# Converting w_out on one line with w_in, and reading it back from DRAM in the first gated pass

## The chip, the cores and the metric

The kernel runs on one core of one Trainium2 chip. The metric is the device time of one execution in microseconds. Three executions of the kernel before took 993.34, 993.7 and 997.28 us; the median is 993.7 us.

## What is computed

Sparse attention over 4 batches and 8 heads (sequence 768, head size 64), and behind it a gated two-layer block over all 3072 tokens (model size 512, hidden size 2048). The mask holds a window of neighbouring blocks of 32, the first and the last block, and three sampled blocks for each row of blocks.

```python
scores = scale * np.matmul(q, k.transpose(0, 1, 3, 2))
scores = np.where(mask, scores, -1000000000.0)
scores = scores - np.max(scores, axis=-1, keepdims=True)
attn = np.exp(scores)
attn = attn / (np.sum(attn, axis=-1, keepdims=True) + 1e-09)
x = np.matmul(attn, v)                      # heads side by side: 3072 x 512
...
h = x @ w_in
g = np.where(h >= 1, h, np.where(h <= -1, 0.0, (h + 1) ** 2 / 4))
out = g @ w_out
```

The weights w_in (512 x 2048) and w_out (2048 x 512) arrive in float64, as 64-bit words.

## The kernel before

**Attention.** The 32 heads follow one another, 12 steps each; a step is one tile of 128 keys by 384 queries. Each head first takes the maximum of its scores: 12 matmuls (L267), 12 reductions on VectorE (L272), a join (L276), a transpose on TensorE (L280) and a product that writes the row of negative maxima into the head's query tile QA (L283). Then come its scores (L303 and L304), the exponential on ScalarE (L308) and the product with v. Heads 0 to 9 are "whole": exponentials go to TensorE in float32 in one matmul (L333). From head 10 on they are split into a rounded part and a rest (L196 on ScalarE, L316 on VectorE), take two matmuls (L335 and L336), and are summed on GpSimd (L323). q and k are loaded (L214), rounded, and moved by DMA into the tiles QA, KA, QB and KB (L221, L237, L238).

**The gated block.** For each batch there are two passes, one for each half of its queries, that run beside the attention of the next batch. A pass goes over 16 slices fi of 128 hidden units, three steps each. The first layer (L457 to L459) multiplies x, in two parts, with w_in's slice, in two parts, from the resident tile wi. Then ScalarE and VectorE form g: L463, L466, L469 (VectorE), a rounding (gh, L196) and a rest (gl, L478, VectorE). The second layer (L485 to L487) multiplies gh and gl with w, the slice fi of w_out, in two parts of 128 x 512.

**Conversions.** Each tile of 128 x 512 float64 weights becomes a float32 pair of a rounded part and a rest. `convert` places three pieces: the load (L162, queue of SP, 512 KB into a tile raw, three buffers), the bits (L168 on ScalarE, then L169, L170, L172 and L174 on VectorE, into a tile cva, two buffers), and the split (a rounding on ScalarE, L196, and a subtraction on GpSimd, L180). There are 16 tiles of w_in and 16 of w_out.

- w_in's tiles stand on a line of their own: one every CSTEP = 5.75 steps from step 8 on. Their split goes into wi.
- w_out's tiles stand in the first gated pass (`first`, batch 0, first half): slice fi is converted shortly ahead of its use, straight into the tile w that the second layer reads, and then stored to a DRAM copy wo_dram (L448, queue of SP, 512 KB). The other seven passes load w back from there (L441), one slice of three steps ahead. The tiles w of conversions and of loads come from one pool of three buffers, wst.

**What sets the order.** Every piece is put into a list with a due time in steps, the list is sorted by it, and the instructions are recorded in that sequence; a scheduler then fixes one order for each engine. Each engine, and SP's queue of DMAs, works in its order: an instruction that waits holds up all behind it.

```python
    for t, load, bits, split in sorted(conv, key=lambda x: -x[0]):
        last = t = min(t, last - P["cd"])
        at(t - P["cl"], load)
        at(t, bits)
        at(t + P["cs"], split)
```

Of the kernel before, what the change touches and what calls it, by code (L numbers as in the profile page):

```python
# [9 lines left out]
F32R = mybir.dt.float32r  # L10
# [12 lines left out]
DM, FF = 512, 2048  # L23
# [14 lines left out]
def body(ctx, tc, qk_t, v, sampled_blocks, moe_w_in, moe_w_out, ind, cm, negd, ident, fold, out):  # L38
# [13 lines left out]
    wst = pool("wst", 3)  # L52
# [13 lines left out]
    Q_KEEP = nc.sync  # L66
# [6 lines left out]
    def f(ap):  # L73
        return ap.bitcast(F32)
# [10 lines left out]
    wi = cst.tile([128, 4, 2, FF], F32R, name="wi")  # L85
# [43 lines left out]
    def at(t, fn, *args):  # L129
        plan.append((t, fn, args))  # L130
# [26 lines left out]
    def convert(t, src, dst, done=None):  # L157
        st = {}

        def load():  # L160
            st["raw"] = cv.tile([128, 512, 2], I32, name="raw", bufs=3)
            Q_RAW.dma_start(out=st["raw"], in_=src.bitcast(I32).rearrange("p (c w) -> p c w", w=2))  # L162

        def bits():
            raw = st["raw"]
            lo32, hi32 = raw[:, :, 0], raw[:, :, 1]
            a = st["a"] = cv.tile([128, 512], I32, name="cva", bufs=2)
            nc.scalar.activation(out=f(a), in_=f(hi32), func=AF.Abs)  # L168
            nc.vector.tensor_scalar(out=f(a), in0=f(a), scalar1=CLO, scalar2=CHI, op0=ALU.max, op1=ALU.min)  # L169
            nc.vector.tensor_scalar(out=a, in0=a, scalar1=3, scalar2=0x3FFFFFFF,  # L170
                                    op0=ALU.logical_shift_left, op1=ALU.bitwise_and)
            nc.vector.scalar_tensor_tensor(out=a, in0=hi32, scalar=-0x40000000, in1=a,  # L172
                                           op0=ALU.bitwise_and, op1=ALU.bitwise_or)
            nc.vector.scalar_tensor_tensor(out=a, in0=lo32, scalar=29, in1=a,  # L174
                                           op0=ALU.logical_shift_right, op1=ALU.bitwise_or)

        def split():
            hi, lo = dst()
            rounded(CH, hi, f(st["a"]))
            nc.gpsimd.tensor_tensor(out=lo, in0=f(st["a"]), in1=f(hi), op=ALU.subtract)  # L180
            if done:
                done()

        conv.append((t, load, bits, split))
# [247 lines left out]
    wo_dram = dr.tile([NF, 128, 2 * DM], F32R, name="wo_dram")  # L432

    def moe(t0, p, b, hf, first):

        g = {}
        G = {**P, **PM} if first else P

        def w_load(fi):
            w = g["w", fi] = wst.tile([128, 2, DM], F32R, name="w")  # L440
            Q_W.dma_start(out=f(w.rearrange("p a d -> p (a d)")), in_=f(wo_dram[fi]))  # L441

        def w_dst(fi):
            w = g["w", fi] = wst.tile([128, 2, DM], F32R, name="w")
            return w[:, 0], w[:, 1]

        def w_keep(fi):
            Q_KEEP.dma_start(out=f(wo_dram[fi]), in_=f(g["w", fi].rearrange("p a d -> p (a d)")))  # L448

        def l1(fi, j):  # L450
            if j == 0:
                last = b == B - 1 and fi % 2
                g["h", fi] = psa.tile([128, 512], F32, name="pa") if last else psh.tile([128, 512], F32, name="hp")
            hv = g["h", fi][:, 0:HALF]
            x = xt[b, j, hf]
            fs = slice(fi * 128, (fi + 1) * 128)
            nc.tensor.matmul(out=hv, lhsT=wi[:, j, 0, fs], rhs=x[:, 0], start=(j == 0), stop=False)  # L457
            nc.tensor.matmul(out=hv, lhsT=wi[:, j, 0, fs], rhs=x[:, 1], start=False, stop=False)  # L458
            nc.tensor.matmul(out=hv, lhsT=wi[:, j, 1, fs], rhs=x[:, 0], start=False, stop=(j == NP - 1))  # L459

        def g_relu(fi):
            r = g["r", fi] = mt.tile([128, HALF], F32, name="r")
            nc.scalar.activation(out=r, in_=g["h", fi][:, 0:HALF], func=AF.Relu, bias=half_c, scale=0.5)  # L463

        def g_sq(fi):
            nc.scalar.activation(out=g["r", fi], in_=g["r", fi], func=AF.Square)  # L466

        def g_max(fi):
            nc.vector.scalar_tensor_tensor(out=g["r", fi], in0=g["r", fi], scalar=1.0, in1=g["h", fi][:, 0:HALF],  # L469
                                           op0=ALU.min, op1=ALU.max)  # L470

        def g_hi(fi):
            gh = g["gh", fi] = mt.tile([128, HALF], F32R, name="gh", bufs=3)
            rounded(nc.scalar, gh, g["r", fi])

        def g_lo(fi):
            gl = g["gl", fi] = mt.tile([128, HALF], F32R, name="gl", bufs=3)
            (nc.gpsimd if first and fi % 4 in GL1 else nc.vector).tensor_tensor(out=gl, in0=g["r", fi], in1=f(g["gh", fi]), op=ALU.subtract)  # L478

        def l2(fi, t):  # L480
            if fi == 0:
                g["o", t] = psc.tile([128, DM], F32, name=f"oa{t}")
            ts = slice(t * 128, (t + 1) * 128)
            gh, gl, w, o = g["gh", fi], g["gl", fi], g["w", fi], g["o", t]
            nc.tensor.matmul(out=o, lhsT=gh[:, ts], rhs=w[:, 0], start=(fi == 0), stop=False)  # L485
            nc.tensor.matmul(out=o, lhsT=gh[:, ts], rhs=w[:, 1], start=False, stop=False)  # L486
            nc.tensor.matmul(out=o, lhsT=gl[:, ts], rhs=w[:, 0], start=False, stop=(fi == NF - 1))  # L487

        end = b == B - 1 and hf == 1
        dst = out[b * S:(b + 1) * S].rearrange("(p t) m -> p t m", t=T)  # L490

        def o_copy(t):
            if t == 0:
                g["out"] = op.tile([128, 3, DM], F32, name="o")
            if end and t == 1:
                nc.vector.tensor_copy(out=g["out"][:, t], in_=g["o", t])
            else:
                nc.scalar.copy(out=g["out"][:, t], in_=g["o", t])
            if end:
                Q_OUT.dma_start(out=dst[:, hf * 3 + t], in_=g["out"][:, t])  # L500

        def o_store():
            if not end:
                Q_OUT.dma_start(out=dst[:, hf * 3:hf * 3 + 3], in_=g["out"])

        for fi in range(NF):
            u = t0 + fi * p
            if first:
                convert(u + 1.5 * p - P["co"], moe_w_out[fi * 128:(fi + 1) * 128, :], lambda fi=fi: w_dst(fi),
                        lambda fi=fi: w_keep(fi))  # L510
            else:
                at(u - p, w_load, fi)
            for j in range(NP):
                at(u + j * p * G["l1"], l1, fi, j)
            m = u + p / 2
            at(m + G["gr"], g_relu, fi)
            at(m + G["gs"], g_sq, fi)
            at(m + G["gm"], g_max, fi)
            at(m + G["gh"], g_hi, fi)
            at(m + G["gl"], g_lo, fi)  # L520
            for t in range(3):
                at(u + G["l2"] * p + t * p * G["l3"], l2, fi, t)
        for t in range(3):
            at(t0 + (NF + G["l2"] - 1) * p + (t + 1) * p * G["l3"] + 0.05, o_copy, t)
        at(t0 + (NF + 1) * p + 0.1, o_store)
# [8 lines left out]
    begin = [PER * H * (b + 1) + DELAY for b in range(B + 1)]  # L534
    p = PER * H / (2 * NF)
    for b in range(NMOE):
        for hf in range(2):
            moe(begin[b] + hf * NF * p, p, b, hf, b == 0 and hf == 0)
    for fq in range(4):
        for kt in range(4):  # L540
            cs = slice(fq * 512, (fq + 1) * 512)
            convert(CONV + (4 * fq + kt) * CSTEP, moe_w_in[kt * 128:(kt + 1) * 128, cs],
                    lambda kt=kt, cs=cs: (wi[:, kt, 0, cs], wi[:, kt, 1, cs]))
    plan_conversions()
    plan.sort(key=lambda x: x[0])
    early = [x for x in plan if x[0] < MANUAL]
# [8 lines left out]
P = {'vw': 4.0, 'r1': 0.857, 'r2': 4.031, 'qs': 9.647, 'ks': 11.666, 'vs': 9.131, 'ld': 5, 'm0': 7.832, 'm1': 5.0, 'mr': 0.46, 'mc': 2.3, 'mt': 1.325, 'mw': 0.9, 'ex': 0.524, 'ph': 1.22, 'pl': 1.349, 'ps': 0.841, 'ow': 0.704, 'ot': 0.2, 'oa': 0.549, 'ah': 0.3, 'al': 0.578, 'su': 0.637, 'de': 1.414, 'yw': 0.799, 'yy': 2.173, 'xm': 0.774, 'xh': 1.0, 'xl': 2.518, 'gr': 0.1, 'gs': 0.279, 'gm': 0.314, 'gh': 0.934, 'gl': 1.232, 'l2': 1.494, 'l3': 0.158, 'l1': 0.121, 'cl': 9.0, 'cs': 1.705, 'cd': 1.8, 'co': 5.196, 'lag': 3.5}  # L555
# [16 lines left out]
NHEADS = B * H  # L572
NMOE = B
PER = 2 * T
CONV, CSTEP = 8.0, 5.75
CLO, CHI = (struct.unpack("<f", struct.pack("<I", w))[0] for w in (0x38100000, 0x47EFFFFF))

_INS = ["qk_t", "v", "sampled_blocks", "moe_w_in", "moe_w_out"]
# [49 lines left out]
```

## Time and profile before

| | |
|---|---|
| median of three executions | 993.7 us |
| the profiled execution, its own time | 991.61 us |
| its span, first to last instruction | 989.8 us |
| TensorE busy | 947.2 us (96%) |
| weight loads (PEld) busy | 830.4 us (84%) |
| VectorE (DVE) busy | 735.9 us (74%) |
| ScalarE (ACT) busy | 637.2 us (64%) |
| GpSimd (POOL) busy | 323.5 us (33%) |
| DMA moved | 154.43 MB |
| first matmul of the gated block (L457) | at 157.2 us |
| conversions on VectorE, first and last | at 20.5 and 284.9 us |

Shares are over the whole span and mix stages with different limits, so they tell little about a change that touches the first 290 us. That stretch is read from sums over parts of it. Matmuls overlap each other, so TensorE's busy time is no measure of how much it could still take; the count of matmuls in a stretch, with the time of one in a stretch where nothing holds TensorE up, is a better one. A row of waits names the engine and line that waited, and what it waited for.

### The profile page before, as it was taken

What the parts mean: (1) busy time and instruction counts of PE and PEld (TensorE: products, weight loads), DVE (VectorE), ACT (ScalarE), POOL (GpSimd) and SP (SyncE); (2) the same over time, 40 slices, a digit from 0 to 9 for tenths busy, and PEclk for the clock granted to TensorE, in tenths of its full rate; (3) what the DMA queues carried; (4) which work ended last, traced back from release to release, by engine and by line L of the source; (5) the groups of instructions that cost most, each with busy time, mean ns of one, the idle gap of its engine ahead of it and who ended that gap; (6) DMA issues with size and microseconds to landing.
All of it is one profiled execution on the core that took longest, in us unless ns stands there. A gap on an engine that the chain in (4) does not pass through costs nothing.

```text
span 989.8 us, 14583 instructions
## 1 busy us (share of the span) xinstructions
PE 947.2 (96%) x4687; PEld 830.4 (84%) x4687; DVE 735.9 (74%) x1349; ACT 637.2 (64%) x1302; POOL 323.5 (33%) x283
## 2 busy tenths in 40 slices
PE   5898899999899999999999999999999999999998
PEld 3666567778779989999989999998999899899996
DVE  5888887679998887888888897888888885422222
ACT  3676666666667666777767676866777676533433
POOL 1222120225554344444544444344544444000000
PEclk9999999999999999999999999999999999999999
DMA  6666676753455454656455454655546442434442
GB/s 196 200 182 184 190 207 204 228 180 103 155 170 172 128 141 129 186 151 174 136 143 175 133 150 137 184 158 152 156 130 187 116 124 86 154 128 128 160 128 96
DMA packets 56216, 154.43 MB, mean 156 GB/s; under 512 B 9612, under 2 KB 17952, under 8 KB 56140
## 3 DMA queue, kind: packets, MB, share of 16 engines
q1 hardware_dynamic: 56100, 153.48, 52.1%
q8 instruction: 37, 0.61, 0.3%
q14 instruction: 39, 0.32, 0.1%
q10 hardware_dynamic: 40, 0.03, 0.0%
HBM read 100.92 MB, written 14.81 MB: 117 GB/s over the span
## 4 chain that ended last, share of the span: by engine, by line
PE 70%; DVE 7%; ACT 2%; issue 1%; POOL 0%; POOLq 0%; ACTq 0%; DVEq 0%
PE oa L485 8%; PE oa L487 8%; PE oa L486 8%; PE hp L457 7%; PE hp L458 7%; PE hp L459 7%; PE po L335 5%; PE pa L303 4%; PE pa L304 4%; PE po L336 4%; PE pa L267 4%; DVE pl L316 2%; DVE mc L272 1%; PE pa L459 1%; PE pa L458 1%
## 5 line engine op out<-in xcount | busy, mean ns | idle before, releaser
L323 POOL TENSOR_TENSOR acc<-acc,pt 128x384 f32<-128x384 f32 x176 | 206.6, 1174 | 189.9 <-ACT pt L308 146.2
L272 DVE TENSOR_REDUCE mc<-pa 128x1 f32<-128x384 f32 x384 | 203.3, 549 | 20.4 <-PE pa L267 17.1
L196 ACT CAST ph<-pt 128x384 fp32r<-128x384 f32 x264 | 135.8, 514 | 94.4 <-PE po L335 90.1
L316 DVE TENSOR_TENSOR pl<-pt,ph 128x384 fp32r<-128x384 f32 x264 | 166.9, 632 | 33.3 <-ACT ph L196 32.4
L308 ACT ACTIVATE pt<-pa 128x384 f32<-128x384 f32 x288 | 140.5, 489 | 49.6 <-PE pa L304 41.6
L457 PE MATMUL hp<-x,wi 128*128 128x384 f32 x448 | 156.3, 349 | 5.4 <-DVE r L469 5.3
L485 PE MATMUL oa<-w,gh 128*128 128x512 f32 x384 | 153.3, 399 | 0.3 <-ACT gh L196 0.3
L459 PE MATMUL hp<-x,wi 128*128 128x384 f32 x448 | 152.1, 340 | 0.0
L458 PE MATMUL hp<-x,wi 128*128 128x384 f32 x448 | 152.0, 339 | 0.0
L487 PE MATMUL oa<-w,gl 128*128 128x512 f32 x384 | 151.5, 394 | 0.0
L486 PE MATMUL oa<-w,gh 128*128 128x512 f32 x384 | 150.8, 393 | 0.0
L267 PE MATMUL pa<-KA,QA 88*128 88x384 f32 x384 | 139.4, 382 | 8.8 <-DMA QA<-qkh 5.9
L469 DVE SCALAR_TENSOR_TENSOR r<-r,hp 128x384 f32<-128x384 f32 x112 | 61.8, 552 | 74.6 <-ACT r L466 74.4
L478 DVE TENSOR_TENSOR gl<-r,gh 128x384 fp32r<-128x384 f32 x128 | 91.0, 711 | 30.2 <-ACT gh L196 28.1
L267 PEld LDWEIGHTS pa<-KA,QA 88*128 88x128 f32 x384 | 73.4, 193 | 33.2 <-DVE mc L272 11.2
L303 PE MATMUL pa<-QA,KA 102*128 102x384 f32 x288 | 99.7, 346 | 0.7 <-DVE mc L272 0.4
L463 ACT ACTIVATE r<-hp,half_c 128x384 f32<-128x384 f32 x112 | 65.1, 581 | 52.3 <-PE hp L459 49.2
L304 PE MATMUL pa<-QB,KB 128*128 128x384 f32 x288 | 98.3, 341 | 0.0
L335 PE MATMUL po<-ph,vn 128*128 128x384 f32 x264 | 91.9, 348 | 4.7 <-DVE xun L345 3.9
L457 PEld LDWEIGHTS hp<-x,wi 128*128 128x128 f32 x448 | 85.0, 190 | 12.3 <-DVE r L469 7.8
L323 POOL TENSOR_TENSOR acc<-pt 128x384 f32<-128x384 f32 x44 | 45.6, 1037 | 136.7 <-ACT pt L308 132.9
L336 PE MATMUL po<-pl,vn 128*128 128x384 f32 x264 | 88.8, 336 | 0.0
(97 smaller groups left out, 1665.7 us busy)
## 6 DMA issues: line engine op xcount, KB each, us to landing
w<-wo_dram SPq DMA_DIRECT2D x112, 512.0 KB
qk<-in_qk_t_dram SPq DMA_DIRECT2D x32, 384.0 KB
raw<-in_moe_w_in_dram SPq DMA_DIRECT2D x16, 512.0 KB
raw<-in_moe_w_out_dram SPq DMA_DIRECT2D x16, 512.0 KB
wo_dram<-w SPq DMA_DIRECT2D x16, 512.0 KB
lv<-in_v_dram SPq DMA_DIRECT2D x32, 192.0 KB
KA<-qkh SPq DMA_DIRECT2D x32, 192.0 KB
QA<-qkh SPq DMA_DIRECT2D x32, 192.0 KB
```

The costliest lines, as they stand in the source:

```text
L267: nc.tensor.matmul(out=pm[:, 0:HALF], lhsT=QAi[0:KM, t * 128:(t + 1) * 128], rhs=KAi[0:KM, kh * HALF:(kh + 1) * HALF], start=True, stop=True)
L272: nc.vector.reduce_max(out=st["mc"][:, t, kh:kh + 1], in_=st.pop(("pm", t, kh))[:, 0:HALF], axis=AX.X)
L308: nc.scalar.activation(out=p, in_=st.pop(("ps", c))[:, 0:HALF], func=AF.Exp, scale=SCALE)
L316: (nc.gpsimd if i < 2 * H and c in PL1 else nc.vector).tensor_tensor(out=pl, in0=st["p", c], in1=f(st["ph", c]), op=ALU.subtract)
L323: nc.gpsimd.tensor_tensor(out=st["acc", hf], in0=prev, in1=st["p", c], op=ALU.add)
L335: nc.tensor.matmul(out=po, lhsT=st["vn"][:, c], rhs=st["ph", c], start=(c == 0), stop=False)
L457: nc.tensor.matmul(out=hv, lhsT=wi[:, j, 0, fs], rhs=x[:, 0], start=(j == 0), stop=False)
L458: nc.tensor.matmul(out=hv, lhsT=wi[:, j, 0, fs], rhs=x[:, 1], start=False, stop=False)
L459: nc.tensor.matmul(out=hv, lhsT=wi[:, j, 1, fs], rhs=x[:, 0], start=False, stop=(j == NP - 1))
L485: nc.tensor.matmul(out=o, lhsT=gh[:, ts], rhs=w[:, 0], start=(fi == 0), stop=False)
L486: nc.tensor.matmul(out=o, lhsT=gh[:, ts], rhs=w[:, 1], start=False, stop=False)
L487: nc.tensor.matmul(out=o, lhsT=gl[:, ts], rhs=w[:, 0], start=False, stop=(fi == NF - 1))
```

## The change

All 32 tiles now stand on one line, one every 4 steps from step 8 on. Each has a key: w_in's four tiles of a quarter of the hidden units have the time one slice ahead of their first use, w_out's tile fi one and a half slices ahead of slice fi, and the line follows the sorted keys: one w_out tile, four of w_in, four of w_out, four of w_in, and so on. A w_out tile is now split into a buffer of wst for the store alone. The first gated pass no longer uses converted tiles directly: like the other passes it loads w from wo_dram, by `w_load`, one slice ahead, which makes 16 more loads of 512 KB. How many conversions there are, and what each consists of, stays.

```diff
@@ -440,13 +440,6 @@
             w = g["w", fi] = wst.tile([128, 2, DM], F32R, name="w")
             Q_W.dma_start(out=f(w.rearrange("p a d -> p (a d)")), in_=f(wo_dram[fi]))
 
-        def w_dst(fi):
-            w = g["w", fi] = wst.tile([128, 2, DM], F32R, name="w")
-            return w[:, 0], w[:, 1]
-
-        def w_keep(fi):
-            Q_KEEP.dma_start(out=f(wo_dram[fi]), in_=f(g["w", fi].rearrange("p a d -> p (a d)")))
-
...
         for fi in range(NF):
             u = t0 + fi * p
-            if first:
-                convert(u + 1.5 * p - P["co"], moe_w_out[fi * 128:(fi + 1) * 128, :], lambda fi=fi: w_dst(fi),
-                        lambda fi=fi: w_keep(fi))
-            else:
-                at(u - p, w_load, fi)
+            at(u - p, w_load, fi)
...
+    def keep(fi):
+        st = {}
+
+        def dst():
+            w = st["w"] = wst.tile([128, 2, DM], F32R, name="w")
+            return w[:, 0], w[:, 1]
+
+        def store():
+            Q_KEEP.dma_start(out=f(wo_dram[fi]), in_=f(st["w"].rearrange("p a d -> p (a d)")))
+
+        return moe_w_out[fi * 128:(fi + 1) * 128, :], dst, store
+
+    tiles = []
     for fq in range(4):
+        cs = slice(fq * 512, (fq + 1) * 512)
         for kt in range(4):
-            cs = slice(fq * 512, (fq + 1) * 512)
-            convert(CONV + (4 * fq + kt) * CSTEP, moe_w_in[kt * 128:(kt + 1) * 128, cs],
-                    lambda kt=kt, cs=cs: (wi[:, kt, 0, cs], wi[:, kt, 1, cs]))
+            tiles.append((begin[0] + (4 * fq - 1) * p,
+                          (moe_w_in[kt * 128:(kt + 1) * 128, cs], lambda kt=kt, cs=cs: (wi[:, kt, 0, cs], wi[:, kt, 1, cs]))))
+            tiles.append((begin[0] + (4 * fq + kt - 1.5) * p, keep(4 * fq + kt)))
+    tiles.sort(key=lambda x: x[0])
+    for n, (_, job) in enumerate(tiles):
+        convert(CONV + n * CSTEP, *job)
...
-CONV, CSTEP = 8.0, 5.75
+CONV, CSTEP = 8.0, 4.0
```

On VectorE the four operations of a conversion change their places among the rest. Before, around the twelfth slice of the first pass, VectorE had these rows (pl is the rest of an exponential, r the hidden layer, xun a head's unnormalised output, cva a conversion):

```order
L316 TENSOR_TENSOR pl<-pt,ph 128x384
L174 SCALAR_TENSOR_TENSOR cva<-raw,cva 128x512
L169 TENSOR_SCALAR cva<-cva 128x512
L469 SCALAR_TENSOR_TENSOR r<-r,hp 128x384
L316 TENSOR_TENSOR pl<-pt,ph 128x384
L345 TENSOR_TENSOR xun<-po,otmp 64x384
L478 TENSOR_TENSOR gl<-r,gh 128x384
L170 TENSOR_SCALAR cva<-cva 128x512
L172 SCALAR_TENSOR_TENSOR cva<-raw,cva 128x512
```

At the same slice the changed kernel has these (its L462 and L471 are the L469 and L478 of before, since the lines behind the removed ones stand seven lines earlier):

```order
L316 TENSOR_TENSOR pl<-pt,ph 128x384 x2
L462 SCALAR_TENSOR_TENSOR r<-r,hp 128x384
L316 TENSOR_TENSOR pl<-pt,ph 128x384
L345 TENSOR_TENSOR xun<-po,otmp 64x384
L471 TENSOR_TENSOR gl<-r,gh 128x384
L316 TENSOR_TENSOR pl<-pt,ph 128x384
```

The four rows of conversions between these are gone from here; they stand earlier. On SP's queue the stores of w_out (L448 before, L536 now) begin among the heads' DMAs of the first batch, and the 16 loads (L441) stand among conversions. TensorE's order is the same but for the first slice, which begins four score tiles earlier.

## The prediction

> **What bounds the kernel now.** I read the slices of the page first, then the sums of each engine over the stretches that differ, then what waited there.
>
> ```profile
> span 989.8 us, 14583 instructions
> ...
> PE   5898899999899999999999999999999999999998
> PEld 3666567778779989999989999998999899899996
> DVE  5888887679998887888888897888888885422222
> ```
>
> One slice is 24.7 us. From the 13th slice on, PE and the weight loads (PEld) stand at 9 or next to it and DVE mostly at 8; before it PEld is at 5 to 8, and DVE at 8 or 9 but for three slices around 175. What the change touches ends at 285 us, so all of it lies in the part where PE isn't the limit. The sums say it closer (columns: length, then busy us and count for PE, PEld, DVE, ACT, POOL, then the granted clock, DMA share and GB/s):
>
> ```profile
> core 0: us, PE busy (x) PEld busy (x) DVE busy (x) ACT busy (x) POOL busy (x), PEclk, DMA share, GB/s
> 20.00:167.00 147.00, 133.03 (x534) 94.64 (x533) 126.43 (x240) 99.45 (x200) 26.22 (x19) 0.99 0.67 193
> 167.00:205.00 38.00, 37.37 (x171) 30.06 (x171) 26.45 (x51) 23.58 (x47) 6.13 (x5) 1.00 0.66 210
> 225.00:285.00 60.00, 54.88 (x263) 47.00 (x263) 58.72 (x97) 38.49 (x82) 30.85 (x25) 0.96 0.42 133
> 285.00:345.00 60.00, 58.47 (x309) 53.72 (x308) 50.27 (x91) 41.89 (x89) 27.32 (x24) 1.00 0.51 155
> 345.00:513.00 168.00, 166.95 (x881) 154.11 (x880) 140.03 (x258) 119.25 (x249) 75.37 (x66) 1.00 0.53 152
> ```
>
> The last row is the regular state: 168 / 881 = 0.191 us for each matmul. By that price the 263 matmuls of 225 to 285 need 50.2 us, so **9.8 us are lost there**, and DVE is busy 58.72 of the 60. In the front (20 to 167) DVE is busy 86%, PEld 64%. Who waits shows it too; the first three rows are of 20 to 167, the last two of 225 to 285 (engine and line, what it waited for, us in total, times, longest):
>
> ```profile
> PEld oa L303 <- DVE QA L283: 8.3, 7, 1.6
> PE oa L303 <- DVE QA L283: 5.5, 6, 1.3
> PE pa L267 <- DMA QA<-qkh: 3.6, 3, 1.3
> ...
> ACT gh L196 <- DVE r L469: 7.0, 6, 2.3
> PEld hp L457 <- DVE r L469: 3.9, 3, 2.5
> ```
>
> In the front PE waits at each head's start for the row of maxima that DVE writes (L283). In 225 to 285 the hidden layer waits for DVE (L469), and the chain of waits in 225 to 290 is made of DVE, with the conversions' four lines (cva) in it:
>
> ```profile
> by line: DVE pl L316 20.5%; DVE mc L272 13.4%; issue 12.3%; DVE cva L172 6.6%; DVE cva L174 6.0%; DVE cva L169 4.8%; DVE cva L170 4.7%; DVE r L469 4.6%; DVE gl L478 4.3%; DVE psum L358 2.6%; DVE xun L387 2.4%; PE hp L457 2.0%; PE hp L458 1.
> ```
>
> **What moves, and its price.** A conversion is four DVE operations, two ACT, one POOL, one load, and for w_out a store. None is added or removed. These rows sum DVE's operations on cva alone (length, busy and count):
>
> ```profile
> 20.00:167.00 147.00, 50.48 (x84) 0.99 0.67 193
> 205.00:285.00 80.00, 22.02 (x28) 0.96 0.47 147
> 225.00:285.00 60.00, 16.85 (x20) 0.96 0.42 133
> ```
>
> One costs 50.48/84 = 0.60 us in the front and 16.85/20 = 0.84 us in 225 to 285, where more of POOL's work stands beside it (30.85 of 60 us busy against 26.22 of 147). In DVE's order 84 of the 128 stand before the first pass's first L469, at about 167 us; of the changed kernel 99 do. Before the sixth L469 (about 203 us) it is 100 and 115; before the eighth (about 223 us) 108 and 124. So **15 operations come into the front**, the stretch 167 to 205 keeps its 16, and 225 to 285 keeps 4 of 20. On paper the line begins one conversion every four steps instead of 5.75, but the two lines together had come to 21 conversions by then already; under 4 are brought forward.
>
> *Gain.* 16 x 0.84 = 13.5 us of DVE work leave 225 to 285. DVE is left with 45 us of work, PE with its 50.2, so PE becomes the limit there as in the row behind it (285 to 345: DVE 84%, 309 matmuls x 0.191 = 58.9 of 60 us). The gain is capped at 9.8; I take **9**. Ends: 4, if half of the loss turns into other waits, and 11.8 (15 x 0.786, all that leaves 205 to 285). The granted clock is part of this: 0.96 in that row, 1.00 behind. The Trainium skill ("TensorE: Matmul & The Clock Gate", What's actually happening) has the gate close after an idle window of some 3.4 us and open under load; by that rule a fed PE gets the 0.04 x 60 = 2.4 us back with the rest, and were the dips due to something else the cap would be 7.4.
>
> *Loss in the front.* Full price: 15 x 0.60 = 9.0 us. At the least nothing, since DVE is idle 147 - 126 = 20.6 us there. At the most 9.8: heads with few and with many of these operations, from one KA move to the next, compare so (operations on cva, then whole engines):
>
> ```profile
> 35.87:54.58 18.71, 7.72 (x14) 0.91 0.59 178
> 140.16:154.29 14.13, 4.91 (x7) 1.00 0.80 239
> ...
> 140.16:154.29 14.13, 13.62 (x57) 9.76 (x56) 13.07 (x24) 10.05 (x21) 1.47 (x2) 1.00 0.80 239
> ```
>
> (18.71 - 14.13) / 7 = 0.65 us for each operation, and the shortest head has DVE at 13.07 of 14.13: a head is about as long as DVE's work in it. (Long stretches hold more operations for other reasons too, so 0.65 is an upper end.) By busy time alone PE would look like the limit of the front, 133 of 147 us, and the loss would be nothing. The Trainium skill ("Perfetto Trace Analysis", Identifying the Most-Contended Engine) says that matmul busy time misleads and that weight loads measure PE; by it PE has a third free (94.64 of 147), DVE is the most contended, the loss is the full 9.0, and more load on DVE there is the wrong way.
>
> What speaks for less than full price is the order itself. Before, this is DVE at the end of head 7's maxima (L272 reduces, L276 joins, L283 writes the row; cva is the conversion):
>
> ```order
> L272 TENSOR_REDUCE mc<-pa 128x1 x3
> L172 SCALAR_TENSOR_TENSOR cva<-raw,cva 128x512
> L276 TENSOR_TENSOR mr<-mc 128x6
> L174 SCALAR_TENSOR_TENSOR cva<-raw,cva 128x512
> L169 TENSOR_SCALAR cva<-cva 128x512
> L283 TENSOR_TENSOR QA_114<-pa,nd 6x768
> ```
>
> And in the changed kernel, same head:
>
> ```order
> L272 TENSOR_REDUCE mc<-pa 128x1 x3
> L276 TENSOR_TENSOR mr<-mc 128x6
> L283 TENSOR_TENSOR QA_114<-pa,nd 6x768
> L372 RECIPROCAL rc<-rc 24x32
> L169 TENSOR_SCALAR cva<-cva 128x512
> L170 TENSOR_SCALAR cva<-cva 128x512
> ```
>
> Three conversion operations stood inside the chain for which PE waits at the head's start, and none does now; over heads 4 to 7 it was 9 and is 0, while 7 now stand between the reduces of heads 3 and 4 and 8 in head 9's chain. 9 x 0.60 = 5.4 us leave the path, one comes onto it at head 8. I credit 4 of them: loss **5**.
>
> *The 16 loads and the ring of three.* A 512 KB load is 0.524 MB; at 193 GB/s for a share of 0.67 (row 20:167) the engines carry 288 GB/s, so 1.8 us each and 29 us in all over some 120 us. The share goes from about 0.55 to 0.75: room is left, and PE's order takes each w as late as before. Tighter is SP's order in the changed kernel, early in the first pass (w_1769 and w_1892 are conversions, w_1798, w_1888 and w_1963 the loads for fi = 2, 3, 4):
>
> ```order
> L441 DMA w_1798<-wo_dram_120 128x1024
> L162 DMA raw_1806<-in_moe_w_in_dram 128x1024
> L384 DMA den_1523<-s2_1790 64x384 x2
> L214 DMA qk_1815<-in_qk_t_dram 128x768
> L441 DMA w_1888<-wo_dram_120 128x1024
> L536 DMA wo_dram_120<-w_1892 128x1024
> L210 DMA lv_1905<-in_v_dram 128x384
> L162 DMA raw_1919<-in_moe_w_in_dram 128x1024
> L221 DMA KA0_115<-qkh_1935 64x768
> L221 DMA QA0_113<-qkh_1935 64x768
> L441 DMA w_1963<-wo_dram_120 128x1024
> ```
>
> Loads that were none now stand between conversions, and with three buffers w_1798 waits for the second layer of fi = 0, w_1963 for the store of w_1892; raw, den, qk and the next head's KA and QA are queued behind. Such waits exist already on SP (first row 157 to 300, second 300 to 400):
>
> ```profile
> SPq L448 <- POOL w L180: 46.6, 12, 9.3
> ...
> SPq L441 <- PE po L336: 17.4, 5, 7.6
> ```
>
> PE never waited for a w behind them. The cost is between 0 and one such wait in full, 9.3 us; with the rows nearer to nothing I take **1**.
>
> Sum: -9 + 5 + 1 = **-3 us** on the profiled execution, 991.61 to 988.6. That execution is 2.1 us under the median of 993.7; from the median it is 990.7. I say 990.
>
> **Rivals.**
>
> *The front takes it for nothing.* The 20.6 idle us of DVE swallow the 15 operations, as the shorter chains suggest. Against it: the heads' lengths follow DVE's work. Then -9 + 0 to +1, up to -10.8: 981 to 985.
>
> *The stores stand in front of the heads' DMAs (slower).* Nine w_out stores now come before head 8's moves on SP, where there was none (w_out used to start at the end of the front). Each waits on SP for POOL's subtraction, 46.6/12 = 3.9 us on average in the row above, and qk loads and QA moves queue behind, in a stage where PE has only the heads to do. If three come through to PE, 3 x 3.9 = 11.7, and the sum is +8.7: 1000 to 1002. It decides as soon as L267's wait for QA moves, 3.6 us now, passes some 10. For it: L267 waits for QA already. Against it: the order places the stores well after their conversions.
>
> *The gain isn't there.* The hidden layer keeps waiting in 225 to 285, for ACT or for w through the ring, and only 4 of the 9 come: -4 + 5 + 1 = +2, 993 to 996. That the change moves too little to be seen belongs here.
>
> **How the numbers follow.** The forecast 0.50 (net -7 to 0), free front 0.22, stores 0.18, no gain 0.10. A difference under 0.5%, 5 us, can't be told from none here. From 993.7, faster by over 5 is the free front and the lower part of the forecast's range: 0.22 + 0.15 = 0.37. Slower by over 5 is the stores case and a little of the others: 0.21. Within: 0.42. Range: down to the free front with the full cap, 982, and up to three stores, 1002.
>
> **What would show it.** Right: DVE's cva operations in the front rise from 84 to 99 and the first L457 comes some 5 us after 157.2; in the 60 us before the end of the first pass PE does over 300 matmuls instead of 263, the clock is at 1.00, and L196's wait for L469 (7.0 us) mostly goes; from there on both kernels run at 0.191 us a matmul. Wrong: the first L457 no later (free front); L267 waiting for QA or PE's L303 for L283 longer than now (stores, DVE); or a wait of the second layer for a w load, which before had none.

## The result, and the profile after

The change made the kernel slower. The changed kernel takes 998.7 us (median of 12 executions, 996.2 to 1006.0), the kernel before 993.0 in the same comparison (12 executions); the ratio is 1.0064, 95% interval 1.0042 to 1.0087. The forecast was 990 (by its sum 990.7, -0.3% from the median); the time moved the other way. The profiled execution of the changed kernel is one of its longest, 1004.5 us with a span of 1002.7, against 991.6 and 989.8 before: of the 13 us between the two profiles some 6 belong to that execution. One execution below, of the run with a ring of four, was slow (1026.7 us at a granted clock of 0.89) and is left out of that run's ratio.

Line numbers behind the diff shift: the first layer is now L450 to L452 (L457 to L459 before), its square L459, the maximum L462 (L469), gl L471, the second layer L478 to L480, a w load L441, the store of w_out L536. The slices of the page first, then the sums by stretches (columns as in the prediction):

```profile
span 1002.7 us, 14602 instructions
...
PE   5988888999999999999999999999999999999998
PEld 4666556678889989999998999998999999999997
DVE  6987877667978778888889888888889785422222
...
PEclk9998998899999999999999999999999999999999
```

```profile
20.00:167.00 147.00, 126.73 (x466) 89.01 (x465) 121.51 (x219) 92.81 (x187) 29.25 (x22) 0.92 0.70 209
167.00:205.00 38.00, 34.85 (x131) 24.93 (x131) 25.94 (x52) 18.63 (x37) 3.85 (x3) 0.88 0.58 189
225.00:285.00 60.00, 57.61 (x285) 50.04 (x283) 51.60 (x91) 42.22 (x86) 26.23 (x21) 1.00 0.59 188
285.00:345.00 60.00, 59.80 (x316) 55.42 (x317) 48.99 (x92) 43.06 (x92) 25.98 (x23) 1.00 0.54 163
345.00:513.00 168.00, 167.02 (x882) 154.37 (x881) 140.38 (x259) 118.98 (x249) 75.55 (x66) 1.00 0.51 151
```

From 345 us on the two kernels are alike (882 matmuls in 168 us, 881 before). In 225 to 285 the gain has come: 285 matmuls instead of 263, DVE at 51.60 instead of 58.72, the clock at 1.00. The front pays more than that: from 20 to 167 PE does 466 matmuls instead of 534, and **DVE too does less, 219 operations instead of 240**, though the change gives it more to do there. Neither engine is full; they wait for each other, and the granted clock is 0.92 and 0.88 in these two rows (0.99 and 1.00 before). The moves of KA on SP time the heads (start, length). First before, then the changed kernel, for the sixth and the tenth move (the expectations call the tenth one head 8's; counted from 0 it is head 9's):

```profile
87.83 0.47 SPq L221 DMA_DIRECT2D KA<-qkh  x1
...
154.29 0.47 SPq L221 DMA_DIRECT2D KA<-qkh  x1
```

```profile
92.21 0.47 SPq L221 DMA_DIRECT2D KA<-qkh  x1
...
176.48 0.47 SPq L221 DMA_DIRECT2D KA<-qkh  x1
```

These four heads, heads 5 to 8 counted from 0, take 66.5 us before and 84.3 in the changed kernel. That is where most of the time went, and the experiments are read by this length; it isn't the whole front, and runs that are alike in it can differ in time. The waits of the front name it in part (changed kernel, 20 to 167; before, L351 6.2, L303 5.5, L280 1.7 and L267 3.6):

```profile
ACT den L351 <- PE oa L333: 11.1, 4, 4.9
...
PE oa L303 <- DVE QA L283: 6.6, 7, 1.1
PE pa L280 <- DVE mr L276: 6.2, 6, 1.6
...
PE pa L267 <- DMA QA<-qkh: 2.8, 2, 1.9
```

### The profile page after: what moved, and what is told of

Read it like the earlier page. It is cut to its first block, busy times and chain, and to the rows that moved or that the text cites. A ratio compares the mean times of both kernels' runs of the same rounds, so it can differ in the third digit from the quotient of the medians.

```text
span 1002.7 us, 14602 instructions
## 1 busy us (share of the span) xinstructions
PE 956.1 (95%) x4687; PEld 837.0 (83%) x4687; DVE 734.8 (73%) x1349; ACT 637.7 (64%) x1302; POOL 321.2 (32%) x283
## 4 chain that ended last, share of the span: by engine, by line
PE 83%; DVE 8%; DMA 4%; ACT 2%; issue 2%; POOL 0%; SPq 0%; DVEq 0%; ACTq 0%; POOLq 0%
PE oa L478 8%; PE oa L480 8%; PE oa L479 8%; PE hp L450 7%; PE hp L451 7%; PE hp L452 7%; PE pa L267 6%; PE po L335 5%; PE pa L303 5%; PE pa L304 5%; PE po L336 4%; PE po L333 3%; DMA QA<-qkh 3%; DVE mc L272 3%; PE oa L333 2%
## 5 line engine op out<-in xcount | busy, mean ns | idle before, releaser
L316 DVE TENSOR_TENSOR pl<-pt,ph 128x384 fp32r<-128x384 f32 x264 | 164.5, 623 | 36.1 <-ACT ph L196 35.1
L450 PE MATMUL hp<-x,wi 128*128 128x384 f32 x448 | 155.4, 347 | 0.8 <-DVE r L462 0.8
L478 PE MATMUL oa<-w,gh 128*128 128x512 f32 x384 | 153.3, 399 | 0.3 <-ACT gh L196 0.3
L480 PE MATMUL oa<-w,gl 128*128 128x512 f32 x384 | 151.4, 394 | 0.0
L452 PE MATMUL hp<-x,wi 128*128 128x384 f32 x448 | 151.3, 338 | 0.0
L267 PE MATMUL pa<-KA,QA 88*128 88x384 f32 x384 | 140.8, 387 | 10.0 <-DMA QA<-qkh 7.8
L462 DVE SCALAR_TENSOR_TENSOR r<-r,hp 128x384 f32<-128x384 f32 x112 | 61.7, 551 | 76.5 <-ACT r L459 76.0
L471 DVE TENSOR_TENSOR gl<-r,gh 128x384 fp32r<-128x384 f32 x128 | 90.5, 707 | 31.6 <-ACT gh L196 29.7
L267 PEld LDWEIGHTS pa<-KA,QA 88*128 88x128 f32 x384 | 74.7, 197 | 34.3 <-DVE mc L272 10.1
L303 PE MATMUL pa<-QA,KA 102*128 102x384 f32 x288 | 100.5, 349 | 2.4 <-ACT pt L308 1.4
L450 PEld LDWEIGHTS hp<-x,wi 128*128 128x128 f32 x448 | 84.5, 189 | 6.6 <-DVE r L462 2.0
```

The costliest lines, as they stand in the source:

```text
L267: nc.tensor.matmul(out=pm[:, 0:HALF], lhsT=QAi[0:KM, t * 128:(t + 1) * 128], rhs=KAi[0:KM, kh * HALF:(kh + 1) * HALF], start=True, stop=True)
L303: nc.tensor.matmul(out=ps[:, 0:HALF], lhsT=KAi[0:KA, ks], rhs=QAi[0:KA, cs], start=True, stop=False)
L316: (nc.gpsimd if i < 2 * H and c in PL1 else nc.vector).tensor_tensor(out=pl, in0=st["p", c], in1=f(st["ph", c]), op=ALU.subtract)
```

## The experiments

Eighteen kernels ran. "Ratio" is against the kernel before, with its 95% interval. The letters in an expectation hold for its own group.

### Parts of the change, one at a time

The question was which part costs the front: DVE's extra work, the nine stores of w_out among the heads' DMAs, the 16 loads with the ring of three, or the start of the line.

Four operations left out of four w_out conversions (slices 1, 4, 6, 8):

```diff
+            if bare:
+                return
...
+        return moe_w_out[fi * 128:(fi + 1) * 128, :], dst, store, fi in (1, 4, 6, 8)
```

> The changed kernel, without VectorE's four operations on four of the w_out tiles (slices 1, 4, 6 and 8): 16 operations less, all in the front, where 83 are left ahead of the first slice's L462 (84 in the kernel before, 99 in the changed one). Loads, stores, ScalarE's and GpSimd's parts of these tiles stay; their values are not w_out's. Theory D (VectorE's work lengthens the front): head 8's KA move, at 154.3 us before and 176.5 changed, comes back to 155 to 160, and the total falls to 984 to 989 us, since the shorter stretch behind it stays short. Theory S (the stores ahead of the heads' DMAs on SP lengthen it): the move stays at 168 or later, the total at 995 to 999.

Measured 996.6 us, ratio 1.0044 (1.0017 to 1.0071): with 16 operations fewer it is 2 us less than the changed kernel, which the intervals don't tell from nothing.

The stores of slices 1 to 9 left out, all loads reading slice 0:

```diff
-        return moe_w_out[fi * 128:(fi + 1) * 128, :], dst, store
+        return moe_w_out[fi * 128:(fi + 1) * 128, :], dst, store if fi == 0 or fi > 9 else None
```

> The changed kernel, without the stores of w_out's slices 1 to 9; all loads of w read slice 0, so the output is not the reference's. VectorE's operations keep their places (100 ahead of the first slice's L462). Theory S: head 8's KA move comes at 155 to 162 us instead of 176.5 and the total falls to 984 to 990. Theory D: the move stays at 170 or later and the total at 995 to 999.

Measured 982.9, ratio 0.9908 (0.9879 to 0.9937). It read like proof that the stores cost 16 us. It isn't, as the last group shows.

The kernel before with the loads of slices 2 to 15 added to the first pass (reading slice 0; the conversions of these slices are only stored):

```diff
-            else:
+            if not first or fi > 1:
                 at(u - p, w_load, fi)
```

> The kernel before, with the loads of the first gated pass added: slices 2 to 15 load slice 0 of the DRAM copy through the same pool of three buffers while the conversions stay in the pass and are only stored, so the output is not the reference's. Front unchanged (80 operations ahead of the first L469). If the loads and the shared pool cost what the changed kernel lost: 997 us or more. If they are hidden, as the prediction had it (1 us): 991 to 995.

Measured 996.4, ratio 1.0042 (1.0009 to 1.0074), where the prediction had +1 us for them.

The line begun later:

```diff
-CONV, CSTEP = 8.0, 4.0
+CONV, CSTEP = 15.0, 4.0
```

> The changed kernel with its line of conversions begun at step 15 instead of 8: 92 operations on cva ahead of the first slice's L462 instead of 99, 6 stores instead of 9 or so in the front, and more conversions in the first pass. Theories D and S both have the front shorter by about half of what it lost: total 990 to 995. If the front's length is set by something else that the change brought (the order of ScalarE, the granted clock alone), 997 to 1000.

Measured 1004.7, ratio 1.0120 (1.0072 to 1.0167). Both theories missed (990 to 995): the loss only moved to later heads (the tenth move of KA at 158.2, the eleventh at 192.1).

### What of a store costs

By then the stores were the suspect: their wait on SP (Q), their bytes on the DMA engines (T), or their bytes ahead of the heads' moves in SP's own queue (R, put on record only with the next group). The first kernel cuts the stores of slices 1 to 9 to 8 columns (loads read slice 0); the next two issue all stores from GpSimd and from ScalarE; the fourth issues them 2.5 steps later:

```diff
+            n = 2 * DM if fi == 0 or fi > 9 else 8
+            Q_KEEP.dma_start(out=f(wo_dram[fi])[:, 0:n], in_=f(st["w"].rearrange("p a d -> p (a d)"))[:, 0:n])
...
-    Q_KEEP = nc.sync
+    Q_KEEP = nc.gpsimd
...
+                at(t + P["cs"] + 2.5, done)
```

> The changed kernel with the stores of w_out's slices 1 to 9 kept at their places in SP's queue, with their waits, but cut to 8 columns each (4 KB instead of 512); all loads of w read slice 0, so the output is not the reference's. Theory Q (a store waits on SP for GpSimd, and the heads' DMAs queue behind it): nothing changes, 995 to 999 us. Theory T (the stores' bytes hold the DMA engines, and the heads' transfers come late): it falls to where the kernel without these stores was, 981 to 987.

> The changed kernel with all stores of w_out issued from GpSimd's queue instead of SP's, so that none waits on SP; same bytes at about the same time. Theory Q: 982 to 988 us. Theory T: 995 to 1000.

> The changed kernel with all stores of w_out issued from ScalarE's queue: off SP too, but ScalarE now waits for GpSimd's subtraction where the store stands in its order. Theory Q: 983 to 992 us, part of the gain given back on ScalarE. Theory T: 996 or more.

> The changed kernel with each store given a due time 2.5 steps (about 4 us) later, so that GpSimd is done when SP comes to it. Theory Q: 984 to 991 us. Theory T: 994 to 1000, the same bytes a little later.

Measured: small stores 989.8, ratio 0.9957 (0.9936 to 0.9978); GpSimd 988.9, 0.9956 (0.9934 to 0.9978); ScalarE 988.8, 0.9958 (0.9938 to 0.9978); late 1001.5, 1.0088 (1.0060 to 1.0116). The second and the third compute all of the reference and are faster than both kernels. But bytes and queue gave the same 9 to 10 us, which neither Q nor T expects. R does, and the late stores fit it too.

The third group tests R: the kernel before with its stores on GpSimd, then the changed kernel with its raw loads taken off SP instead (stores on SP, GpSimd, ScalarE):

```diff
-    Q_KEEP = nc.sync
+    Q_KEEP = nc.gpsimd
...
-    Q_RAW = nc.sync
+    Q_RAW = nc.gpsimd
```

> Control: the kernel before, with its stores of w_out issued from GpSimd's queue. Its stores lie in the first gated pass. If stores on SP are only dear where the heads stand alone (theory R below), 990 to 994 us; if moving stores off SP helps anywhere, 984 to 989.

> The changed kernel, its stores left on SP, but the loads of the raw weights (32 of 512 KB) issued from GpSimd's queue. Theory R (what delays a head is the bytes that stand ahead of its moves in SP's own queue, whoever put them there): as much gain as from moving the stores or more, 983 to 991. Theory Q (the stores' waits on SP): no gain, 995 to 1001.

> The changed kernel with stores and raw loads both on GpSimd's queue. Theory R: SP carries only the heads' own transfers and the loads of w, 980 to 987 us. Against it: GpSimd works its queue in order too, and a raw load that waits for VectorE would hold its subtractions; then 988 to 996.

> The changed kernel with the stores on ScalarE's queue and the raw loads on GpSimd's. Theory R: 980 to 987 us, as with both on GpSimd; if GpSimd's order is what limits that one, this is the better of the two by 2 us or more.

Measured 995.7, ratio 1.0028 (1.0008 to 1.0048); 998.2, 1.0054 (1.0035 to 1.0073); 1003.6, 1.0113 (1.0084 to 1.0142); 1007.9, 1.0143 (1.0109 to 1.0176). Fewer transfers on SP don't help as such. With the raw loads on GpSimd the second KA move comes at 27.2 to 28.9 us instead of 21.0, a loss at the second head already, so these three tell little of the stores. Heads 5 to 8 are short in them (69.7 to 74.4 us); they lose again behind, with the twelfth KA move at 226.5 to 239.9 (209.5 before).

### The square: bytes, waits and order

All kernels so far had one thing in common that none of the theories named: Tile's scheduler can lay the program out anew when a store's size, place or queue changes. So one kernel was sought that changes a store and nothing in any engine's order. A store of 512 KB that reads the first converted block of w_in, where no wait for GpSimd is left, has the changed kernel's order on every engine; cut to 8 + 8 columns it has that of the run with small stores. The third issues the first one's bytes from ScalarE, the fourth is the changed kernel with four buffers for w; in the first three all loads read slice 0.

```diff
+                Q_KEEP.dma_start(out=f(wo_dram[fi]).rearrange("p (a d) -> p a d", a=2), in_=f(wi[:, 0, :, 0:512]))
...
-    wst = pool("wst", 3)
+    wst = pool("wst", 4)
```

> The changed kernel with the stores of slices 1 to 9 at their places on SP and with their 512 KB each, but read from the first converted block of w_in instead of from w, so that none waits for GpSimd (wo_dram gets wrong slices, and all loads read slice 0). Every engine's order is that of the changed kernel. Theory Q (the wait of a store holds what is queued behind it on SP): nearly all of the 16 us between the changed kernel (998.7) and the kernel without these stores (982.9) goes, 983 to 990. Theory B (their bytes ahead of the heads' moves in SP's queue): nothing goes, 996 to 1000. Both together: 990 to 996.

> The same, cut to 8 + 8 columns each: neither bytes nor waits; the order is that of the run with small stores that wait (989.8). Theory Q: the 7 us between that run and the kernel without the stores are its waits and go, 982 to 985. Theory B: the waits cost nothing, 988 to 991, and the 7 us belong to the other order of the kernel without stores.

> As the first of this call, with the bytes issued from ScalarE's queue instead of SP's, no waits. If bytes cost by standing ahead in SP's own queue: 985 to 991. If they cost by loading the engines, whichever queue issues them: as the first of this call, 996 to 1000 under theory B. Under Q: 983 to 990, as the first.

> The changed kernel with four buffers for w instead of three: loads and conversions wait less for a buffer. If the ring of three has a part in the loss (up to the 4 us of the run with loads only): 994 to 996. If not: 997 to 1000.

Measured 998.7, ratio 1.0052 (1.0031 to 1.0073); 989.1, 0.9952 (0.9930 to 0.9975); 992.2, 1.0002 (0.9979 to 1.0026); 998.1, 1.0049 (1.0019 to 1.0078). **The waits of the stores cost nothing that can be told**: without them the first is where the changed kernel is, and the second where the small stores with waits are. Nor does the ring of three: with four buffers every engine's order is the changed kernel's up to 215 us, and so is the time. The third has an order of its own (the table below). Bytes or order was left.

The last two change the size of the nine stores in the program that the scheduler has already ordered: the changed kernel's order without the bytes, and the second kernel's order with them (the edit is shown for the latter).

```diff
+    names = {KEPT[fi].ins.name for fi in range(1, 10)}
+    wide = lambda x: _copy.replace(x, ap=[[s, 512 if n == 8 else n] for s, n in x.ap])
+    for block in nc.main_func.blocks:
+        block.instructions = [_copy.replace(d, ins=(wide(d.ins[0]),), outs=(wide(d.outs[0]),)) if d.name in names else d
+                              for d in block.instructions]
```

> The changed kernel, every engine's order and every wait as there; only the stores of slices 1 to 9 are cut to 8 columns after the order has been made (wo_dram keeps most of these slices unwritten, and all loads read slice 0). Theory B (the stores' bytes delay the heads): as the two runs without these bytes, 988 to 991. Theory S (the scheduler lays the front out differently as soon as a store's size, place or queue changes, and the order of the changed kernel is the slow one; bytes cost little): as the changed kernel, 996 to 1000.

> The kernel without bytes and without waits (989.1), its order on every engine kept, with its nine stores widened to 512 KB each after the order has been made (they still read the first converted block of w_in; all loads read slice 0). Theory B: as the changed kernel, 996 to 1000. Theory S: as the kernel whose order it has, 988 to 991. Between: each has a part, and these two runs with the two of the call before give both.

Measured 997.0, ratio 1.0056 (1.0032 to 1.0080), without the bytes; 989.1, 0.9957 (0.9940 to 0.9974), with them. So it is the order: 997.0 to 998.7 in the one, with or without bytes and waits, 989.1 to 989.8 in the other.

### What the two orders do

The moves of KA without the bytes in the changed kernel's order, then with the bytes in the other order:

```profile
89.56 0.47 SPq L221 DMA_DIRECT2D KA<-qkh  x1
...
173.77 0.47 SPq L221 DMA_DIRECT2D KA<-qkh  x1
```

```profile
86.20 0.50 SPq L221 DMA_DIRECT2D KA<-qkh  x1
...
164.03 0.47 SPq L221 DMA_DIRECT2D KA<-qkh  x1
```

84.2 and 77.8 us for the same four heads (the first profile is of one of that run's longer executions, 4 us over its median). Below, DVE in one of them (the changed kernel, seventh KA move at 110.05; its block of conversions began at 109.16; columns: start, length, engine, line, operation, idle time before it):

```profile
113.00 1.78 DVE L172 SCALAR_TENSOR_TENSOR cva<-raw,cva 128x512 int32<-128x512 int32 x1
114.82 0.69 DVE L174 SCALAR_TENSOR_TENSOR cva<-raw,cva 128x512 int32<-128x512 int32 x1
115.43 0.42 DVE L169 TENSOR_SCALAR cva<-cva 128x512 f32<-128x512 f32 x1
115.88 0.43 DVE L170 TENSOR_SCALAR cva<-cva 128x512 int32<-128x512 int32 x1
116.34 1.78 DVE L172 SCALAR_TENSOR_TENSOR cva<-raw,cva 128x512 int32<-128x512 int32 x1
118.16 0.69 DVE L174 SCALAR_TENSOR_TENSOR cva<-raw,cva 128x512 int32<-128x512 int32 x1
118.77 0.55 DVE L387 TENSOR_TENSOR xun<-xun,den 128x384 f32<-128x384 f32 x1
119.24 0.55 DVE L272 TENSOR_REDUCE mc<-pa 128x1 f32<-128x384 f32 x1
...
124.18 0.56 DVE L272 TENSOR_REDUCE mc<-pa 128x1 f32<-128x384 f32 x1 [1.00 <-PE pa L267]
125.49 3.01 DVE L272 TENSOR_REDUCE mc<-pa 128x1 f32<-128x384 f32 x6 [0.75 <-PE pa L267]
128.53 0.17 DVE L276 TENSOR_TENSOR mr<-mc 128x6 fp32r<-128x6 f32 x1
129.01 0.95 DVE L283 TENSOR_TENSOR QA<-pa,nd 6x768 fp32r<-6x768 f32 x1 [0.32 <-PE pa L280]
```

And the same head in the other order with bytes (seventh KA move at 105.43):

```profile
106.16 0.69 DVE L172 SCALAR_TENSOR_TENSOR cva<-raw,cva 128x512 int32<-128x512 int32 x1
...
114.05 0.69 DVE L174 SCALAR_TENSOR_TENSOR cva<-raw,cva 128x512 int32<-128x512 int32 x1
114.65 6.15 DVE L272 TENSOR_REDUCE mc<-pa 128x1 f32<-128x384 f32 x12
120.84 0.17 DVE L276 TENSOR_TENSOR mr<-mc 128x6 fp32r<-128x6 f32 x1
120.92 0.42 DVE L169 TENSOR_SCALAR cva<-cva 128x512 f32<-128x512 f32 x1
121.38 0.43 DVE L170 TENSOR_SCALAR cva<-cva 128x512 int32<-128x512 int32 x1
121.95 0.95 DVE L283 TENSOR_TENSOR QA<-pa,nd 6x768 fp32r<-6x768 f32 x1
```

In the changed kernel three conversions, 12 operations, run in one block ahead of the head's first reduce; in the other order it is ten. In this head the first reduce starts 9.2 us after the move in both. PE in the changed kernel's order (the run without bytes, same order, same head, seventh KA move at 107.38):

```profile
117.17 0.44 PE L267 MATMUL pa<-KA,QA 88*128 88x384 f32 x1 [0.92 <-DVE mc L272]
118.39 1.28 PE L333 MATMUL oa<-pt,vn 128*128 128x384 f32 x2 [0.77 <-ACT xun L353]
119.17 0.81 PE L267 MATMUL pa<-KA,QA 88*128 88x384 f32 x1
119.78 1.48 PE L333 MATMUL oa<-ph,vn 128*128 128x384 f32 x2
```

L267 waits until a reduce has freed its bank, then takes turns with the L333 of the head before, and the reduces in their turn wait for PE. The row L283 starts 19.0 us after the KA move. In the other order two operations of a conversion stand **inside** the chain, ahead of L283, and the row still comes 16.5 us after the move: the reduces ran without a gap.

This head doesn't show where most of it is lost. Summed over heads 5 to 8, from one row L283 to the next, the stretch from the first reduce to the row takes 33.4 us in the changed kernel and 34.6 in the other order with bytes (31.8 before); the stretch ahead of the first reduce takes 51.3 and 40.7 (36.1 before). There VectorE waits for ScalarE's first operation of a conversion (L168), and the reduces stand behind that wait. The rows of DVE in 105 to 157, first the run without bytes in the changed kernel's order, then the other order with bytes:

```profile
DVE cva L169 <- ACT cva L168: 5.5, 4, 3.2
```

```profile
DVE cva L169 <- ACT cva L168: 1.0, 1, 1.0
```

Over the four heads this wait is 8.2 us in the changed kernel and 1.8 in the other order with bytes; the runs whose stores don't wait give nearly the same, 8.7 and 2.5. So some 6 of the 10.6 us between the two orders are this wait. It doesn't make an order slow by itself, as the kernel before has 6.3 of it in these heads. PE in 107 to 157 (first the one without bytes in the changed kernel's order, then the other):

```profile
107.00:157.00 50.00, 42.84 (x148) 29.47 (x147) 39.66 (x68) 29.85 (x61) 9.13 (x7) 0.86 0.56 161
```

```profile
107.00:157.00 50.00, 42.44 (x163) 29.79 (x162) 44.76 (x77) 34.30 (x71) 11.74 (x9) 0.95 0.77 238
```

As busy, but 148 matmuls against 163, at a clock of 0.86 against 0.95, with the DMAs at 0.56 against 0.77: the faster one moves more bytes. Counted out of each kernel's order (conversion operations ahead of the first reduce, and between it and L283, summed over heads 5 to 8; PE's other matmuls ahead of the first L267, where one L333 stands for the two that a profile shows), beside the length of these heads from the KA moves:

```
kernel                               cva ahead  inside  PE ahead  heads 5-8, us
before                                  31        6        81        66.5
stores on GpSimd                        26       22        63        71.0
no stores of slices 1 to 9              26       23        65        71.5
stores on ScalarE                       22       28        69        72.6
bytes without waits, on ScalarE         34       14        82        73.2
small stores / no bytes, no waits /
  bytes in that order                   39        9        93     77.8 / 77.3 / 77.8
changed, 16 operations fewer            40        1       122        79.3
late stores                             43        5       117        81.8
bytes without waits / ring of four /
  no bytes in that order / changed      48        1       119     82.2 / 82.6 / 84.2 / 84.3
```

Below the first row each has 48 to 50 of these operations but the one with 16 fewer (41). Where they are spread through the chain, these heads are 4.5 to 6.1 us longer than in the kernel before; where they stand in blocks ahead of it, 16 to 18. The columns move together, so the table shows what goes with what and no cause; nor does it carry over to the whole time, for stores on GpSimd or ScalarE (988.9, 988.8) end where the other order does (989.1). That the order decides is shown: within each of the two orders bytes and waits change nothing, and from one to the other, at the same bytes, the time moves by 9.6 us (998.7 and 989.1). Which row of it (DVE's blocks, the waits for ScalarE's L168 in them, or PE's late L267) wasn't tried alone, and stays open.

## Why the prediction was wrong, by its own steps

The front and what lies behind it are told apart by the first layer: the first matmul of its sixth slice (L457, 196.7 us before) and of its 21st (318.5). In the run with the changed kernel's order and stores that don't wait, whose profile lies near its median, these come at 215.3 and 325.1; in the other order without bytes, profiled at its median, at 207.2 and 316.4; in the changed kernel's own long profile at 222.9 and 332.6.

- *The gain behind the front, 9 us.* Right in kind, and too small. The lag falls from 18.6 to 6.6 us, by 12.0, in the one order, and from 10.5 to -2.1, by 12.6, in the other; the changed kernel's profile gives 12.2. The upper end was 11.8. The signs came: 1.00 of the clock, DVE no longer full, and the hidden layer's wait nearly gone (225 to 285, 7.0 us before):

```profile
ACT gh L196 <- DVE r L462: 1.7, 2, 0.9
```

  The matmuls there rose to 285 (296 in the other order with bytes; 294 in the changed kernel's own last 60 us of the first pass, 239 to 299), short of the 300 that were named.
- *The loss in the front, 5 us.* **This is the step that failed.** It was priced by the count of operations, less a credit, and measured 18.6 us in the changed kernel's order. The count came as read: 99 conversion operations stand ahead of the first slice's maximum, 84 before. The credit was "Three conversion operations stood inside the chain for which PE waits at the head's start, and none does now; over heads 4 to 7 it was 9 and is 0", and "I credit 4 of them". It weighed the operations behind the last reduce and not those ahead of the first. In heads 5 to 7 all of them stand ahead now, twelve in a block, and that order is the slow one. What the prediction saw come in ("7 now stand between the reduces of heads 3 and 4 and 8 in head 9's chain") it put at nothing: between a head's first reduce and its row, over heads 3 to 9, there are 18 operations in the changed kernel and 11 before.

  But the credit is only 4 us of the miss. No price by the count gives 18.6 and 10.5 us for the same 15 operations: the full 9.0 is near the other order and half of the changed kernel's. PE's order wasn't read, though the first L267 of head 7 had moved from behind 15 other matmuls to behind 34, nor were VectorE's waits for ScalarE's L168. The sign it gave for itself was the first layer some 5 us after 157.2. It came at 171.8 in the changed kernel, and at 161.0 in the other order with bytes (there the second slice is 10.6 us late, at 180.5):

```profile
L450 PE MATMUL hp<-x,wi x448: 332/337/637, 171.8 to 989.1; 128*128 128x384 f32 x150
```

```profile
L450 PE MATMUL hp<-x,wi x448: 332/337/637, 161.0 to 976.1; 128*128 128x384 f32 x150
```

- *Loads and the ring, 1 us.* A fourth buffer changed nothing that can be told (1.0049 against 1.0064), and PE waited for no w. The loads alone, put into the kernel before, took 1.0042, but under an order of their own: not settled.
- *The rival with the stores.* It gave the time nearly (1000 to 1002), by a mechanism that doesn't act, which is luck. Neither the waits nor the bytes of the stores cost anything that can be told, and its sign stayed out: L267's wait for QA is 2.8 us in 20 to 167, far from 10.
- *The full price.* The prediction cited the Trainium skill ("Perfetto Trace Analysis", Identifying the Most-Contended Engine) for a rule that gave the full 9.0. The loss was 18.6 us in one order and 10.5 in the other, with the same load on DVE, and in the changed kernel DVE did fewer operations in the front than before (219 against 240): the runs bear out that PE wasn't the limit there, not that DVE's load set the time.

The net of -3 us is near what the other order gives, 989.1 and 989.8, -0.4% to -0.5%. That is luck: there the loss is 10.5 us, where 6 were forecast with the loads, and the gain 12.6, where it was 9.

## What to carry to other kernels

Where a scheduler lays out the program, a kernel with one thing taken out is another layout, and its time is no price of that thing: here the same work took 989 or 998 us by the layout, and the first groups of runs blamed the stores for it. Keep the order word for word (compare it on every engine), or change the instruction after it has been ordered. And an operation that leaves the inside of a chain hasn't left the path: in the slow order hardly any stood inside, and the time was lost ahead of the first link. Read what stands there, and what it waits for, on each engine that takes part, and don't price operations by their count alone.

## What the runs showed of the hardware that wasn't expected

The transfers had slack where the prediction feared for them: nine stores of 512 KB more or less between the heads' moves on one queue changed the time by less than 2 us in either order (997.0 and 998.7; 989.1 and 989.1), with the DMA share at up to 0.77 in the window above. And an operation's own length isn't that of the mean (0.60): in the block above two of the L172 took 1.78 us each, where L174 beside them took 0.69. Both ran beside GpSimd's subtraction L180 (from 112.95 and 116.29, 1.28 and 1.29 us). In the profiles of the kernel before, the changed kernel and the other order with bytes 27 of a conversion's VectorE operations took over 1 us, and each of the 27 ran beside an instruction on GpSimd; many others that did so stayed short.
